# Another written order for a fused attention, gated bilinear and mixing kernel: exps, scores, adds, pieces and their banks

## The chip, the cores and the metric

The kernel runs on one core of a Trainium2 chip. The metric is the device time of one execution in microseconds. Three runs of the kernel before gave 643.65, 643.19 and 643.61 us, with a median of 643.61 us.

## The reference

The input x has 2,048 rows of 512. Attention with 32 heads of width 16 and a bilinear unit with 1,376 hidden columns work on the same x, and a gate per row mixes the two.

```python
def _A_ref(x, wqkv, wo):
    qkv = (x @ wqkv).reshape(B, S, 3, H, Dh).transpose(2, 0, 3, 1, 4)
    q, k, v = qkv[0], qkv[1], qkv[2]
    scores = jnp.einsum("bhqd,bhkd->bhqk", q, k) * (Dh ** -0.5)
    p = _softmax(scores, axis=-1)
    o = jnp.einsum("bhqk,bhkd->bhqd", p, v)
    return o.transpose(0, 2, 1, 3).reshape(B, S, D) @ wo

def _B_ref(x, w_gate, w_up, w_down):
    h = (x @ w_gate) * (x @ w_up)
    return h @ w_down

g = _sigmoid((x * gate_w).sum(-1, keepdims=True))
return g * _A_ref(...) + (1 - g) * _B_ref(...)
```

## The kernel before, in words

**Tiles and units.** Queries are handled in four chunks of 512 columns and heads in four groups of eight. A pass m (0 to 31) is one chunk, one group and every second head of the group, so four heads j. Keys come in 16 tiles kt of 128. A unit (m, kt, j) is one block of scores, 128 keys by 512 queries of one head; there are 2,048 of them. The scores of a unit are one matmul on a 32-row strip of TensorE, into a PSUM bank of its own (`do_row`, L786). An exp then turns the bank into a cell of the SBUF buffer `PT`, which has 58 cells of 512 columns (`do_exp`). ACT does 1,300 units with its exponential (L863). DVE does the other 748 as an integer addition whose result, read as a float of 16 bits, is a power of two with a straight line between the powers (L865). Two shifted copies of such a cell, which POOL makes with an integer addition (`do_add`, L883), are weighted into the value product, so that the error of the straight line averages out. An exp or an add can take two units in one instruction (three for ACT), if their banks are neighbours and their cells have one spacing; an add is a pair of instructions, one for each copy.

**Value products.** `do_pv` (L831) adds probabilities times values: four matmuls of 128 rows, one on each 32-column strip, for the four heads of the pass, into bank 7. There are 888 such rows with 3,544 matmuls: 2,048 with a plain cell and 1,496 with a shifted copy. The sums of the probabilities come out of the same products. Afterwards bank 7 is copied out (task `oc`), the sums are inverted and spread (tasks `dn`, `rc`, `rg`, `re`, `rb`) and multiplied in (task `mu`).

**Pieces.** Projections of x (names q, k, v, z), the bilinear unit (u, g) and the output (o) are works of several pieces each. A piece is four matmuls on the four column strips (`do_fill`, helper `mm_col`, L702). The work takes a bank with its first piece and gives it back when its result is copied out. A few pieces are instead cut in four row quarters and put among scores (L781).

**Order.** Nothing on the chip chooses the order. `SCHED` (L220 and following) is a packed text with one line for each operation. The loop behind L1115 unpacks it and gives each line to its function. The order of the lines is the order of each engine's instructions. Waits follow from the data: each operation carries what it depends on, and `_Plan.emit` writes the semaphores. `take_cell` (L848) makes an exp or an add wait for the last readers of a cell that it overwrites, and `bank_rel` makes a score or a first piece wait for the exp or copy that read its bank. The lines are:

- `R 0 m kt j bank`: scores of a unit (L786); `R 1 name piece quarter ...` is a quarter of a piece (L781).
- `F name piece [bank]`: a piece (L702).
- `V m a b c d`: a value product, with the key tile and the copy for each head (L831).
- `E engine m kt j cell ...`: an exp of one to three units (L863 for ACT, L865 for DVE).
- `A n ...`: an add of n units into 2n cells (L883).
- `T name engine`: a copy, a small operation or a DMA (`run_task`). `S` and `C` are three matmuls at the end.

At the end, after the last value product, DVE transposes bank 7 and inverts the sums (tasks `tx`, `tr`, `tg`, `ty`), TensorE spreads them with the selection matmuls `S` (L1143), DVE multiplies them in (tasks `tt`, L1098), and the last pieces of the four output works o30 to o33 (the sixteenth, with `Qr`) use the result.

Of the kernel before, what the change touches and what calls it, by code (L numbers as in the profile page):

```python
# [17 lines left out]
AX = mybir.AxisListType  # L18
# [186 lines left out]
def bass_gated_mix__mha_block__glu_gated_bilinear__prompt_kernel(  # L205
# [19 lines left out]
    "^*31uYUlTV??>?{*8y5}CDiW@`SjztkY=n{T(83SJ6%JF)?)qt=Oncy+TM@d3-#~!-Yf5I!WW>5iHHZdF#G}h>+^j7k3BSzuWkIXg3p4qNp%VdpTZ)p<VEMFL3|(j#TNXQk$i&|*u7$~"
    "adF_!z#lNDb0giizj+iOM**^Aou7i@w{@(6YilUJ9R<$&+BE6rdwQMC&KblF`oY!UU*lh|-WnY%NF*WZ#dHNV^%Q=;wfM?BV|w0o`+T?gUO(S#<a;@M0#$b|tULeM_t1X)e}DGAQ;h2R"
    "iF97j=7nF54HYjy^DdlPL46l%c&{73V{kA02B2s9ePcd#i<b_W@NX21n29?%==0%5_2i#{KicZ|R+uOq!ELxmT*&Zk=<JuUdVc$ENXHppujWDTN2}S|+umB$KrHxCThTbU@8#BdC_1b-"
    "OKc~FvwrE3Ss&ab`RR&Td1@hkU+z=)1ny&(JZhW#rit%=-&hSc6xhxy@PGTB*M)z4J_M^xrz4QrWAVb|Q&c-B3pB1Uf|2sm+q`1--I@bnW$rHtjF-If)?e`KsC)4CllL#hj=T4Q7Y*hw"
    "uh08<HtKbYJ@bh*>7NwSoU7EiYF(%+hP!&~LgOlrJ@wY0a1m>5-&OJXDM)Z~xPeU{R|o$(|0+^ruVden2(%K;M)3QyuDyY^U<^rh@2q8`3+pG?iof{r*g=9ozTbQTWh5AjACKNm(U{-t"
    "`kQ@Je=Wog7cvi_#rwuZFpL-HcK`CemI>ZbEZ_;#7f=TizTb@%KREvq=ywHti%8$C@%acb&3ZX~U+?QFz@OHGY4L2R?070YELj*Y)$Riu<T%5B?&$>)kiMk*B6-~UrGZKEet{pzy@U0S"  # L230
    "`AH5m>#y<ehz?%-egAg80%Ow1=#eeiEnoU0!Hn3Mn+jvlhQaItQM`BQ*n*T^5LWE6G0G<>$lqm)Uk?5qI;!JcDev4&nWvO?68pW2kEvueMHmUZSaAe@NoAdN{|)0K(qc^f`L3;c@ICil"
    "4aAt{%Q5Tz-P8(ppmc~FJHd(x;&j2IzpSms`~qz_Y7PpIe}t@#zX$&&*04msC8zII`n>=hGR*f6?{N?ax?_#h><-0A^Q)n<E{G@&rDL1hdl!eIg^3mRuDvI~xFGzlm&U#yeM@t3Zvp0f"
# [24 lines left out]
    "tfde&8Y6H){PmyQ?SFeeOZ6O<q&X}o#u)$xMriL}BhOvGjf6JTE3Y<cvYiR1m!2vQy;MT;E|B?o=-7C~-HA1@1X*S7o+09%H3%>KUP5OlwUaX)w5zF$Qfut-z3#)W`j%Tu6XsN(2f*gl"
# [215 lines left out]
T, KD, NCH, NB, FT = 16, 4, 4, 4, 11  # L473
# [816 lines left out]
```

## Time and profile before

| | |
|---|---|
| median of three runs | 643.61 us |
| span of the profiled execution | 641.4 us |
| PE busy | 634.8 us in 8,804 matmuls |
| ACT busy | 622.1 us in 837 instructions |
| DVE busy | 597.0 us in 927 instructions |
| POOL busy | 514.7 us in 1,185 instructions |
| granted TensorE clock | 1.000 |

The profiled execution's span runs from its first to its last instruction; its own device time is not listed apart from the three runs, which are 1.8 to 2.3 us longer than the span. PE is TensorE's matmuls and PEld its weight loads, which overlap the matmuls. A group's busy time leaves overlaps out, while its mean is that of single instructions, start to end. In the view of waits, an idle time names what ended it.

### The profile page before, as it was taken

The page shows a single profiled execution, that of the slowest core. Times are in us where ns is not written, and L with a number is a line of the kernel's source. Part 1 is how long each engine was busy: PE and PEld are TensorE (multiplying, and loading weights), DVE is VectorE, ACT ScalarE, POOL GpSimd, SP SyncE. Part 2 cuts the span into 40 slices and gives each one's busy share as a digit, 9 for nine tenths or more (in the row PEclk, how much of TensorE's full clock was granted, in tenths as well). Part 3 has the DMA queues.
Part 4 walks back from the last instruction along what each step waited for, and adds up shares of the span by engine and source line. Part 5 has one row for each costly group of instructions (what it writes and reads, how often), then busy time and mean ns, then how long its engine had stood idle before and what let it go on. Part 6 is the DMA issues. An engine that isn't in the chain of part 4 may idle for free.

```text
span 641.4 us, 21177 instructions
## 1 busy us (share of the span) xinstructions
PE 634.8 (99%) x8804; PEld 202.4 (32%) x8804; DVE 597.0 (93%) x927; ACT 622.1 (97%) x837; POOL 514.7 (80%) x1185
## 2 busy tenths in 40 slices
PE   8999999999999999999999999999999999999997
PEld 3333232223323322333232333323333223333233
DVE  6999999999999999999999799999998999999975
ACT  6999999999999999999999999999999999999994
POOL 2469899897978889797998789878688998888862
PEclk9999999999999999999999999999999999999999
DMA  8930211001010010101001010100101000000001
GB/s 154 287 100 3 68 15 31 17 6 30 12 28 4 20 43 3 37 10 34 4 11 38 10 43 12 30 9 5 33 4 44 19 23 16 4 26 3 28 20 37
DMA packets 30803, 21.17 MB, mean 33 GB/s; under 512 B 18632, under 2 KB 26540, under 8 KB 30704
## 3 DMA queue, kind: packets, MB, share of 16 engines
q1 hardware_dynamic: 29200, 18.75, 11.3%
q8 instruction: 69, 1.13, 0.7%
q10 hardware_dynamic: 1504, 1.05, 0.7%
q14 instruction: 30, 0.25, 0.1%
HBM read 11.64 MB, written 2.37 MB: 22 GB/s over the span
## 4 chain that ended last, share of the span: by engine, by line
PE 93%; DVE 4%; DMA 1%; ACT 1%; issue 0%; ACTq 0%; DVEq 0%
PE ps L831 35%; PE ps L786 29%; PE ps L702 28%; DVE PT L865 2%; DMA wa<-in_A_wqkv_dram 1%; ACT PT L863 1%; PE ps L781 1%; DVE wa L1027 0%; DVE usb L1019 0%; ACTq L559 0%; DVE QE L904 0%; DVE oc L904 0%; PE ps L1143 0%; DVE rec L1064 0%; DVE rec L1061 0%
## 5 line engine op out<-in xcount | busy, mean ns | idle before, releaser
L863 ACT ACTIVATE PT<-ps 128x1024 bf16<-128x1024 f32 (+2 forms) x823 | 615.3, 886 | 4.9 <-PE ps L786 2.6
L883 POOL INT64_ADD PT<-PT x1174 | 511.8, 457 | 113.7 <-DVE PT L865 73.2
L865 DVE TENSOR_SCALAR PT<-ps 128x512 int16<-128x512 f32 (+1 forms) x641 | 467.9, 773 | 26.7 <-PE ps L786 21.2
L831 PE MATMUL ps<-PT,V 128*32 128x512 bf16 (+1 forms) x2048 | 262.3, 384 | 0.0
L831 PE MATMUL ps<-PT,VS 128*32 128x512 f16 x1496 | 242.8, 384 | 0.0
L786 PE MATMUL ps<-QE,KK 32*128 32x512 bf16 x2048 | 237.4, 384 | 0.9 <-ACT PT L863 0.3
L786 PEld LDWEIGHTS ps<-QE,KK 32*128 32x128 bf16 x2048 | 64.8, 91 | 230.5 <-ACT PT L863 126.0
L831 PEld LDWEIGHTS ps<-PT,V 128*32 128x32 bf16 x2048 | 63.9, 95 | 62.6 <-issue 49.5
L831 PEld LDWEIGHTS ps<-PT,VS 128*32 128x32 bf16 x1496 | 59.2, 94 | 49.2 <-issue 32.1
L702 PE MATMUL ps<-xT,wg 128*32 128x512 bf16 x704 | 51.9, 382 | 0.1
L702 PE MATMUL ps<-xT,wu 128*32 128x512 bf16 x704 | 52.0, 382 | 0.0
L702 PE MATMUL ps<-wd,wa 128*32 128x512 bf16 x668 | 50.7, 382 | 0.0
L1027 DVE TENSOR_TENSOR wa<-ps,usb 128x512 bf16<-128x512 f32 x44 | 30.1, 685 | 1.3 <-PE ps L702 0.8
L1019 DVE TENSOR_TENSOR usb<-ps,omg 128x512 bf16<-128x512 f32 x44 | 30.1, 684 | 1.0 <-PE ps L702 0.7
L702 PEld LDWEIGHTS ps<-xT,wg 128*32 128x32 bf16 x704 | 15.5, 95 | 18.1 <-issue 6.3
L904 DVE COPY oc<-ps 128x512 f32<-128x512 f32 x31 | 21.1, 682 | 0.0
L702 PE MATMUL ps<-xT,wa 128*32 128x512 bf16 (+1 forms) x272 | 20.6, 379 | 0.5 <-DMA wa<-in_A_wqkv_dram 0.5
L702 PEld LDWEIGHTS ps<-wd,wa 128*32 128x32 bf16 x668 | 14.8, 95 | 19.1 <-issue 9.6
L702 PEld LDWEIGHTS ps<-xT,wu 128*32 128x32 bf16 x704 | 14.9, 95 | 17.9 <-issue 6.3
L702 PE MATMUL ps<-wo,OT 128*32 128x512 bf16 x240 | 19.9, 382 | 0.0
L702 PE MATMUL ps<-wa,xT 128*32 128x512 bf16 x256 | 18.1, 381 | 0.3 <-DMA wa<-in_A_wqkv_dram 0.3
L702 PE MATMUL ps<-xT,wq 128*32 128x512 bf16 x256 | 18.0, 388 | 0.0
(85 smaller groups left out, 148.2 us busy)
## 6 DMA issues: line engine op xcount, KB each, us to landing
rb<-rscr SPq DMA_DIRECT2D x16, 256.0 KB
QE<-Qr SPq DMA_DIRECT2D x120, 16.0 KB, 1.8
oc<-oc SPq DMA_DIRECT2D x60, 32.0 KB, 1.9
out_dram<-ost SPq DMA_DIRECT2D x12, 128.0 KB, 1.9
wu<-in_B_w_up_dram SPq DMA_DIRECT2D x1, 1376.0 KB, 7.2
wg<-in_B_w_gate_dram SPq DMA_DIRECT2D x1, 1376.0 KB, 11.8
wd<-in_B_w_down_dram SPq DMA_DIRECT2D x1, 1280.0 KB, 15.1
wa<-in_A_wqkv_dram ACTq DMA_DIRECT2D x1, 512.0 KB, 7.0
```

The source lines that it names most:

```text
L702: r = pe.matmul(ps[32 * i : 32 * i + 32, bank, 512 - x_.shape[1] : 512], w_, x_, start=s0, stop=s1, tile_position=(0, 32 * i), skip_group_ ...
L781: w.op = pe_op(lambda pe, lhs=lhs, rhs=rhs, r=r, q=q, bank=bank, s0=s0, s1=bool(last): pe.matmul(ps[:, bank, :], lhs[r, :], rhs[r, :], sta ...
L786: o = pe_op(lambda pe, b=b, kt=kt, j=j, p=p, bank=bank: pe.matmul(ps[:, bank, :], KK[32 * j : 32 * j + 32, b, kt * 128 : kt * 128 + 128], ...
L831: return pe.matmul(ps[32 * j : 32 * j + 32, OB, :], lhs, rhs, start=s0, stop=s1, tile_position=(0, 32 * j), skip_group_check=True)
L863: o = P.op("act", lambda a: a.activation(PT[:, cs, :], ps[:, bs, :], ACT.Exp, scale=math.log(2.0) / 1024.0), deps)
L865: o = P.op("dve", lambda v: v.tensor_scalar(PT[:, cs, :].bitcast(I16), ps[:, bs, :], BIAS16, 0.0, ALU.add, ALU.max), deps)
L883: return g.int64_add(PT[:, zl, :].bitcast(I64), PT[:, src, :].bitcast(I64), PH[r] * 0x0001000100010001)
L904: return lambda v: v.tensor_copy(dst, src) if scale is None else v.tensor_scalar(dst, src, scale, None, ALU.mult)
L1019: return fill_op(key, "dve", lambda v: v.tensor_tensor(usb[:, i % 2, :], ps[:, bank, :], omg[:, cf, :], ALU.mult), d)
L1027: return fill_op(key, "dve", lambda v: v.tensor_tensor(hT[:, f, :], ps[:, bank, :], usb[:, i % 2, :], ALU.mult), d)
```

## The change

Only the text in `SCHED` is new; no function is touched. As a diff it is 256 packed lines taken out and 242 put in, of which nothing can be read. Unpacked, the orders have 6,374 and 6,259 lines. The operations of each kind:

| | before | after |
|---|---|---|
| exps on ACT of one, two, three units | 363, 443, 17 | 468, 392, 16 |
| exps on DVE of one, two units | 534, 107 | 508, 120 |
| units on ACT, on DVE | 1300, 748 | 1300, 748 |
| adds of one, two units (two instructions each) | 426, 161 | 122, 313 |
| scores | 2048 | 2048 |
| value products, their matmuls | 888, 3544 | 888, 3544 |
| pieces whole, quarters | 780, 52 | 781, 48 |
| tasks | 552 | 552 |

733 of DVE's 748 units are the same, the pieces keep their order within some 15 places, and scores stand some 20 places from where they stood among the scores. Nearly every value product joins other key tiles. Each exp and each add has new cells: in the order before, a cell is used again long after its last reader, in the new one often right behind it.

The packed lines look like this in the diff:

```diff
 SCHED = (
...
-    "{rFo_z~}4V{{hrjDW?"
...
 )
```

Unpacked, the first lines that differ:

```diff
-E act 0 0 2 0 0 0 0 1
+E act 0 0 2 0 0 0 0 57
...
-E act 0 0 1 2 0 0 3 3
+E act 0 0 1 55 0 0 3 56
...
-E act 0 2 1 13 1 0 0 14
-E dve 0 1 2 15
-F k01 1 6
+E dve 0 1 2 3
+E act 0 3 3 6
```

Adds in pass 7, before and after:

```
A 1 7 4 1 33 17
A 1 7 1 2 1 4
```

```
A 2 7 1 3 7 7 0 27 56 42 48
```

The end, from the last value product to the last sixteenth piece, before (two lines that the steps of the end speak of are the `S` lines and `F o31 15`):

```
V 31 43 39 45 22
T tx dve
F o33 0
T oc31 act
T tr dve
T tg dve
T ty0 dve
T dn31 sp
T ty1 dve
F o32 14
...
S 0 4
S 1 3
T tt0 dve
T tt1 dve
F o33 3
F o33 10
F o30 15
F o31 15
F o32 15
F o33 7
F o33 6
F o33 15
F o33 5
```

and after:

```
V 31 38 45 45 -
T tx dve
F o33 5
T ce4 dve
T tr dve
T tg dve
T oc31 act
T ty0 dve
F o33 10
...
S 0 4
T dn31 sp
T ty1 dve
S 1 3
T tt0 dve
F o31 15
T tt1 dve
F o30 15
F o33 6
F o32 15
...
F o33 15
F o33 13
```

More of the change, by code (lines that the diff above doesn't have):

```diff
@@ L225 @@
[L225 to L232, printed above, removed]
@@ L469 @@
[L469 to L470 removed]
+    "c-n0JTdplRjxC7(S1V=*jzgp*dwlxGJq<`4tpAFLja@(@)5|?8&IO|NwTxqs9JaII8$QjJnMo8ykrc(p|NQ(p#>YO#|M5TLYVz0lJHCJa{ki|x_tpRP8K2F+<P+oX{6GHJ=g0Ra|L5l)|NF;t{qN89"
+    "|M~a-hkyTD{Qcj)TX_ES?;i5nKC7;ucJg|D_l0(%ng8GOe}0@V@AJF&|NXo=aAEl2-7|{+ZQmUjE`~H>pS`o2<LT%7{f5v2C;!G5MnUV}cN2~A$G_YB{*K@5Rb5O%`h2o6Dtqu)qy5Ig_XxAU2j~Y1"
+    "3n;#7h%prB6n$Uh7|@nwI|@eNC1FoY8z8K{A53RU>_6V#?8ou*OzVHyZzE^*`%k#~{v$yBe(m{g;KK0Jn0|WNyFhpd==bV!fB$Qc8Z|LE0dIVkH2D4ARpXnl8Sokvo*e*Z29X-E_*@PCI)7)NJU-#X"
@@ new lines @@
+    "8~!VZ=BFpo2`MHZ$n?7xVq-mj1m#-)ZQ#f8)3^_+Ib{eFlbLhuNj%>;5TZPucMAruWwQez4?HXS?ry%nzn{)`;5m`BW0|3Mv~=O6i66($2=uJ)Zs+HY=C`btGdj%~u}@C-uJvpm&`5UsfZv0DzTbhM"
+    "BT$}iJp;BT_@{{jZ%zF08<#o%{=x#lLjc^-c>>bQ`7Dga{C?x*yS+2kWp?_E;T90aLwxbp#19ytf5?2!7-f#@8=7Y}{%h4@d0sU^|My+bT|>5Ftoe7V`8_`KqZs*y`IOeaKLj<N#YVor_RlTr;sDD7"
+    "D9+zmKtDaNha>*i*~|WUB^x}xTeI(0bCwU8{T0h0LG?oJ@e9$}v+lpKb$#qb75?yw9Ni(biKgvYS3m#%f90~eK%W=p;vx&ZWah7@*_v&yH3RX2>+6&2|Ni(hW8eRO+Ph;u8k+AREMZFDsCV|Trp&oN"
+    "6d0d7ekPDv%;4^o3(5KbeZQ9L15)DDqN~0!A%JLLSq*StffyKV;uS3nz5gEZB`|;gVev!f@8oZBK$F!REqdYD>#aK_RlL3w&~IWrsvR&98;KKBN%}N0PyTuG7wc?>NX&seJ<nA%*0gs8@9(J_xyp=#"
@@ new lines @@
+    "FL0gg(pvD^74-f6|4ZSwXVo-_-(x-qk_kZbp<w)Z@;5lZ&H0bTG=)Ns_f(Hh3rnwQUmuEA^MGDvGDK)ElKDCL-r%qE7bN~YvN;|ypQCUvdy>64W!#u>!cb+lEY|Nf3h)`Em(T8B=q)6s(Bt#=H~j_P"
+    "o3T8veJ`JH2DC~?aLmT{y;D#?;(cTH8|w2JMLzNrpWhhymK@(RG}z3;ho`-iBnNALy8Z6(`OkUxu>5bfOoiZk_Wb!*>u>9H?a~UK1*H01$pf3I#2G1J6<hr;^X3W$IwE}0*a8gSK+Wgh=4-8oD9)qH"
+    "T`=z5>sA!2S$r>^s4R-nZ13Sbya32uf%g;W@jJdGx?+O9r_DfS>%*<U189%3*ZCq^mQrzmI14@#{U;gGQax{hg~<2*P4)?E&BoK&4k}rE81oJW^9}YxLgOKm7)kJ_?|**w^bVa-<#-QDV^zO)4I>p{"
+    "+adg9nR-fQTZId1S(f_M(?1A%DW%Q_xy@nhSz5{RTD=d{2{GEI7x;Kj^LV)HGcl`}(sMmtBIpP~mJNq`_UEH0hm!OsRp&pcN<Y8Gu|S@EUp%|EFHY+D2uqtfg%$*LLwwd4RQJN|!Vc0D(Ls=<W!jrI"
@@ new lines @@
+    "0)KdR%Z@TyGi5>#?E>-N%;I_$+BZ>sv61Ur+JDao6kmU+{+mLVDu$Mu7XwEV9?|M%z;l#_eM3dVvlaaHTS(Xty_c<R=ab3b(KI|$0(~=D54bHkW-Qz5kxl>W^N(+=eSi30|2JE3B?5n_iY>1EHWtM9"
+    "(C31Pjuz}`;dd^a;E80&#uXZC?VACQ;NN!*_G#8Fk>Itj+Om`$w%1c+qLzi!kZ-IvT`RZC|88%hMbn<``sNr$V4=1-fh2I(?@4_m&h;#bU;`&-dxA8+iD2!AKo%I@_f60NbiV4<p1I%v{OX>bF?f-;"
+    ">8`DpsD<7zi=LlF{e^k_?*4luYsCy=0~=572c!qBlTW6O&LCa?`1>!|31L|Kokr*t_$;)~26A&j)^KJsUV!?LgXlfRy>%#bU);TaZyDlxhE8u+txj)^vS`A{c5>>1{CMrS{_*dYj4S>;`xSG{bn4L$"
+    "t;>GNDEb4*w=7G?Mk@EgVzaS9YK!KlHg9Pw3W#@%F-Y(Zj{dZ3;496nW?}uTy@`Qb*}(Ns<apzGhQ5Wj&Uo#3+Wmfa0c$ZcN?eIr=Z-hWcES>nGhl@D5#gY7K=F{5e?k{~X4AQ~c&<#)_6y;8>K*>s"
@@ new lines @@
+    "op)*KRv~6>EjiSobAQs&tA#NOR2~prUuY{ToWVZ1Q5R6XEBDKf;#D!$vg{hZjAbu5vI)W25bTe?$jlf}#fH*d>uL`PFtenx(4Bmi^=@Y>D#0TwW5UDlevw-n+qdq@vH+g)mx+`x0Zd&Kc&;nOx(yS$"
+    "@Ma7eHj@=#$=R+{ZL=<;XP6t(;{|O>JL9DcdQ-vbFt%inyWE;~B%bWiPURq&rlSCzrt>#5G-l^&Dom%V`A$<B6l~PieRexbhFo%R=VANJLpo!0Zm}z*$GDrsM8coxkg{o5GYt~otS_C|and;KS@sr3"
+    "bipNbr>KFJx<FFRF8`mou{;u55^x5tb0MFit#pEJ+mfg~ggR1Q(Wy4&&Zf0(o<c#c&MK@It4mTB=*&3IO~$d(4F<r6XjYUB=Ip+;7IC8DN>JzB(yPeu_-GpK>^;4lwb-9!6~NzRf^wyVG9>mj^kHXq"
+    "u-*$f*Ej+@IkYIW5Os1Ou3ql(=)CFo$Y4CaI`X1Et^qRdOEW`z*&gDoz4-59sQizgCTTyd3VsIzxmmhAE=OL}UzBCf&nzm&;rtT0alAr!ce-|iwcH&NPoyQrU}f4aMtB04W}Pz&frTZs%7)tUk<=^)"
@@ L471 @@
+    "W$ni6nm_w;C%Z2f6~B0UV~FwXKRfy2M%dr1_jo<;ew?@W;~xr2<@o"
 )
```

457 lines of the change are left out of this document (216 added, 241 removed).

## The prediction

> **What bounds the kernel now.** I read the page's first part and the chain that ended last, then the groups by shape, then PE's timeline.
>
> ```profile
> span 641.4 us, 21177 instructions
> PE 634.8 (99%) x8804; PEld 202.4 (32%) x8804; DVE 597.0 (93%) x927; ACT 622.1 (97%) x837; POOL 514.7 (80%) x1185
> PE 93%; DVE 4%; DMA 1%; ACT 1%; issue 0%; ACTq 0%; DVEq 0%
> PE ps L831 35%; PE ps L786 29%; PE ps L702 28%; DVE PT L865 2%; DMA wa<-in_A_wqkv_dram 1%; ACT PT L863 1%; PE ps L781 1%; DVE wa L1027 0%; DVE usb L1019 0%; ACTq L559 0%; DVE QE L904 0%; DVE oc L904 0%; PE ps L1143 0%; DVE rec L1064 0%; DVE rec L1061 0%
> ```
>
> 93% of the chain is PE: the value products (L831), the scores (L786) and the pieces of the projections (L702). ACT is busy nearly as long, so it is a second bound close behind. Busy shares do not tell which of them gives way, because matmuls overlap; the distances between PE's starts do.
>
> ```profile
> 300.16 0.38 PE L831 MATMUL ps<-PT,V 128*32 128x512 bf16 x1
> 300.48 0.39 PE L786 MATMUL ps<-QE,KK 32*128 32x512 bf16 x3
> 300.80 0.39 PE L831 MATMUL ps<-PT,V 128*32 128x512 bf16 x2
> 301.02 0.39 PE L831 MATMUL ps<-PT,VS 128*32 128x512 f16 x4
> 301.36 0.40 PE L786 MATMUL ps<-QE,KK 32*128 32x512 bf16 x4
> 301.69 0.40 PE L831 MATMUL ps<-PT,V 128*32 128x512 bf16 x4
> 301.93 1.05 PE L702 MATMUL ps<-xT,wu 128*32 128x512 bf16 x16
> ```
>
> Two kinds of work alternate. A column step is four matmuls on four column strips (a row V, or a piece F). A score stretch is a run of rows R on different row strips. From column step to column step it takes 0.22 us (300.80 to 301.02; the four steps at 301.93 last 1.05, less one matmul of 0.39 gives 0.22 for each of three). Into a stretch it takes 0.32 (300.16 to 300.48), out of it 0.32 (300.48 to 300.80), and a stretch of three scores costs what one of four does (301.36 to 301.69 is 0.33). So PE's time is a count of steps and of stretches, not of matmuls; I use 0.216 and, for a stretch with both its edges, 0.642.
>
> The written order before has 1,094 steps from column to column, 572 stretches, and 31 second rounds inside longer stretches, where a row strip comes again (one more step each). That is 1,094 x 0.216 + 572 x 0.642 + 31 x 0.21 = 236.3 + 367.2 + 6.5 = 610.0 us.
>
> ```profile
> 6.13 1.40 PE L702 MATMUL ps<-xT,wq 128*32 128x512 bf16 x16
> 632.07 0.38 PE L831 MATMUL ps<-PT,VS 128*32 128x512 f16 x1
> 633.79 0.60 PE L702 MATMUL ps<-wo,OT 128*32 128x512 bf16 x8
> 634.33 1.13 PE L1143 MATMUL ps<-usb,sel 128*128 128x256 f32 x4
> 635.39 0.61 PE L702 MATMUL ps<-wd,wa 128*32 128x512 bf16 x8
> 635.83 0.82 PE L702 MATMUL ps<-wo,Qr 128*32 128x512 bf16 x12
> 637.12 0.39 PE L702 MATMUL ps<-wd,wa 128*32 128x512 bf16 x4
> ```
>
> From the first piece at 6.13 to the last at 637.12 are 631.0 us; less 610.0, and less 1.4 for the selection matmuls (634.01, which is 633.79 and a step, to 635.39), some 19.6 us are left. This leftover, 3% of the span, is all the waiting that PE does, and all that any reordering without fewer stretches can win.
>
> **The change, part by part.** The count of units, of value products and of tasks stays. What moves are the counts below, read from the two written orders.
>
> PE. Steps go from 1,094 to 1,097, stretches from 572 to 570, second rounds from 31 to 30: +3 x 0.216 - 2 x 0.642 - 0.21 = -0.85 us. At the end, after the last value product, 17 pieces follow in place of 18 and the selection comes after eleven of them in place of nine, so that its DVE result is needed directly: the sixteenth piece of o31 stands right behind the second selection matmul. Before, two plain pieces at 635.39 stood between.
>
> ```profile
> 635.06 0.86 DVE L1098 TENSOR_TENSOR Qr<-ps,oc 128x256 bf16<-128x256 f32 x2 [0.52 <-PE ps L1143]
> ```
>
> The first of these two products starts 0.73 after the selection's first matmul (634.33) and lasts 0.43 (half of 0.86): 1.16 plus a handover of some 0.05 as an estimate from the gaps above, against 1.06 (634.33 to 635.39) after which PE is free. So PE waits 0.15 there, and the PE part is -0.85 + 0.15 = -0.7 us.
>
> Exps. ACT's singles go from 363 to 468, doubles from 443 to 392, triples from 17 to 16; DVE's singles from 534 to 508, doubles from 107 to 120. Units per engine stay at 1,300 and 748.
>
> ```profile
> L863 ACT ACTIVATE PT<-ps 128x1024 bf16<-128x1024 f32 x443 | 428.1, 1064 | 3.2 <-PE ps L786 2.0
> L863 ACT ACTIVATE PT<-ps 128x512 bf16<-128x512 f32 x363 | 201.5, 638 | 1.7 <-PE ps L786 0.6
> L863 ACT ACTIVATE PT<-ps 128x1536 bf16<-128x1536 f32 x17 | 25.6, 1506 | 0.1
> L865 DVE TENSOR_SCALAR PT<-ps 128x1024 int16<-128x1024 f32 x107 | 130.2, 1219 | 3.8 <-PE ps L786 3.2
> L863 ACT ACTIVATE PT<-ps 128x512 bf16<-128x512 f32 x10 | 5.0, 641 | 0.0
> L863 ACT ACTIVATE PT<-ps 128x1024 bf16<-128x1024 f32 x17 | 15.8, 1061 | 0.0
> 130.25 3.07 DVE L865 TENSOR_SCALAR PT<-ps 128x512 int16<-128x512 f32 x5
> ```
>
> The means overstate it, for instructions overlap their successors. In two stretches of like exps back to back (fifth and sixth row), ten singles take 5.0, so (5.0 - 0.64) / 9 = 0.48 each, and seventeen doubles 15.8, so (15.8 - 1.06) / 16 = 0.92 each. ACT's own load becomes 105 x 0.48 - 51 x 0.92 - 1 x 1.38 (a double and half of one) = +2.1 us. By the groups' busy time (201.5 / 363 = 0.555, 428.1 / 443 = 0.966, 1.506) it would be +7.5, but that counts waiting starts as work; I take 2.1, since ACT does run back to back (it idles 5.0 us before all 823). DVE: singles are (3.07 - 0.68) / 4 = 0.60 apart, so -26 x 0.60 + 13 x 1.217 = +0.2: nothing. The Trainium skill, "Perfetto Trace Analysis", section "Optimizing Scalar/DVE Operations", gives a fixed cost per instruction on PSUM data of about 51 ns for Scalar and 125 ns for DVE. By it ACT would gain 53 x 0.051 = 2.7 us of load and DVE lose 1.6. The trace agrees for ACT (2 x 0.48 - 0.92 = 0.04) and not for DVE (2 x 0.60 - 1.217 is below zero).
>
> On the path, ACT's 2.1 us is costed at nothing, because ACT's own sum lies below PE's: 363 x 0.48 + 443 x 0.92 + 17 x 1.38 = 605 us before, 607 after, inside the 621 between first and last exp (below). If that cover is gone, it costs 2.1.
>
> ```profile
> L863 ACT ACTIVATE PT<-ps x823: 592/1020/1612, 9.5 to 630.9; 128x1024 bf16<-128x1024 f32 x90, 128x512 bf16<-128x512 f32 x71, 128x1536 bf16<-128x1536 f32 x4
> ```
>
> Banks and the leftover. PE waits where a bank's exp ends late.
>
> ```profile
> PEld ps L786 <- ACT PT L863: 126.0, 310, 0.8
> PEld ps L786 <- DVE PT L865: 61.5, 151, 0.6
> PEld ps L786 <- issue: 26.2, 67, 0.4
> PEld ps L831 <- POOL PT L883: 8.4, 36, 0.5
> ```
>
> Most of these idle times are the plain edge of a stretch: 0.391 us where nothing held it (26.2 / 67), against 0.407 with an exp named (187.5 / 461). The excess is 461 x 0.016 = 7 us, the part of the leftover that exps cause at a stretch's first score; the rest sits inside stretches, at the start and in tenths of steps. Which sign does the new order give it? I counted, in both orders, how many of the some 2,045 bank returns leave under 0.05 us beyond the shortest chain (score 0.38, exp, two handovers): 309 before, 329 after. Doubles on DVE are the cause: 185 of theirs were that tight, 208 are. If the whole leftover went with tight returns, that is 20 / 309 x 19.6 = +1.3 us. If it went with returns of one engine and margin at the trace's rate for them, the split ones, which come back sooner, offset the doubles: -0.2 to +0.4. I take +0.1, since the excess named above is only a third of the leftover.
>
> Adds. POOL's instructions fall from 1,174 to 870: 122 single and 313 double pairs in place of 426 and 161.
>
> ```profile
> L883 POOL INT64_ADD PT<-PT x1174 | 511.8, 457 | 113.7 <-DVE PT L865 73.2 <-DVE OT L1078 21.1 <-PE ps L831 7.0
> ```
>
> POOL idles 113.7 us before its adds, so at most 304 x 0.457 = 139 us less work there is worth nothing. A merged pair delivers its first copy later, by up to one add's 0.457; the cover is the distance in PE's order from the scores to the product that reads a copy, whose shortest twentieth rises from 2.9 to 3.1 us. Without that cover the price is the 36 waits above, 8.4 us with their edges, doubled at worst.
>
> Cells. 181 exps now write a cell of PT whose last reading value product stands behind their own scores; before it was 2. They wait one edge (0.32) longer than for the scores, if the engine is idle then. ACT idles 5.0 us over 823 exps, so it is at the previous exp still; zero is taken, and 181 x 0.32 = 58 us of delayed starts is what is uncovered if the engines were waiting.
>
> Sum: -0.7 + 0.1 = -0.6 us on a span of 641.4. The three runs had a median of 643.61 us; the 2.2 between lies around the recorded instructions and is untouched by the order. So 643.61 - 0.6 = 643.0.
>
> **The rivals.** *ACT becomes the bound (slower).* Its place is every stretch in which ACT's load exceeds PE's steps, its price 2.1 us, and it decides if ACT's 14 us beyond its sum (621 - 607) cannot be spent because each gap is shorter than an exp. For it: ACT idles 5.0 us in all. Against it: PE holds 93% of the chain, ACT 1%. PE's saving then counts for nothing: 643.61 + 2.1 = 645.7. The same section of the Trainium skill advises grouping operations when the engine is saturated, and "TensorEngine Tiling (Array Packing)", section "PSUM Bottleneck", says that PSUM copies may become the limit once tiling has sped up TensorE; splitting goes against both, and the trace bears them out as far as ACT's 97%.
>
> *Sooner returns shrink the waiting (faster).* 51 more doubles are split, and a split exp gives its first bank back 0.43 us (1.064 - 0.638) sooner. If a third of the 7 us goes, the time is 643.61 - 0.7 - 2.3 = 640.6. For it: 461 stretches stood behind an exp. Against it: the count of tight returns does not fall.
>
> *The reordering touches nothing* (643.6): margins are equal and waits are jitter of exps. It falls into the forecast's own range.
>
> **How the numbers follow.** What runs of this kernel can tell from no change is about 0.2%, 1.3 us: 642.3 to 644.9. The forecast with its bounds, -0.7 - 0.2 to -0.7 + 1.3, is 642.7 to 644.2 and lies inside; chance 0.44. Sooner returns 0.33, ACT as the bound 0.23. The range reaches from 640.4 (640.6 and the 0.2 that the returns may give) to 646.1 (645.7 and the 0.4 that they may cost); what is left out is a halving of the waits, and ACT at its busy-time price of 7.5.
>
> **What would show it.** In the profile after, ACT's singles keep 0.48 and doubles 0.92; the excess of stretches behind an exp stays at 7 us, give or take 2; PE keeps over 90% of the chain; POOL's idle time grows past 113.7 without PE waiting for it more. Wrong would be: ACT taking several per cent of the chain, stretches waiting longer than 0.407 behind ACT, or exps waiting for L831, which this trace does not show.

## The result and the profile after

The kernel after takes 647.25 us (median of four runs, 646.33 to 648.37) against 643.61 us before. The ratio is 1.0058 with a 95% interval of 1.0044 to 1.0072, so it is slower by 3.6 us, or 0.6%. The forecast of 643.0 us had the sign wrong, and the range (640.4 to 646.1) misses the median by 1.15 us. The profiled execution took 647.01 us. The lines of the code stand 14 earlier than before (L863 is now L849, L865 L851, L883 L869, L831 L817, L786 L772, L702 L688, the product `mu` L1064, and the DMAs on SP: `od` L1041, `re` L1055, `rb` L1060, `dq` L961).

The first part of the page after, and its chain that ended last:

```profile
span 644.3 us, 21223 instructions
PE 634.8 (99%) x8804; PEld 198.0 (31%) x8804; DVE 597.0 (93%) x914; ACT 624.2 (97%) x890; POOL 466.2 (72%) x881
PE 76%; ACT 13%; SPq 3%; DMA 3%; DVE 3%; issue 1%; ACTq 0%; POOL 0%; DVEq 0%
PE ps L817 27%; PE ps L688 25%; PE ps L772 24%; ACT PT L849 13%; SPq L961 2%; DVE PT L851 1%; DMA oc<-oc 1%; DMA wa<-in_A_wqkv_dram 1%; DMA rscr<-rec 1%; SPq L1041 1%; PE ps L767 1%; SPq L1060 0%; SPq L1055 0%; DVE OT L1064 0%; ACTq L545 0%
```

PE is as busy as before, to the tenth, in a span 2.9 us longer. But it holds 76% of the chain where it held 93%. ACT's exps went from 1% to 13%, and new names are SP's queue and the DMAs behind it: `oc<-oc` (task `od`) and `rscr<-rec` (task `re`), with the issues of `dq`, `od`, `rb` and `re`. The view of groups by shape shows ACT's load:

```profile
L849 ACT ACTIVATE PT<-ps 128x1024 bf16<-128x1024 f32 x392 | 384.5, 1095 | 2.2 <-PE ps L772 1.7
L849 ACT ACTIVATE PT<-ps 128x512 bf16<-128x512 f32 x468 | 257.5, 663 | 3.9 <-PE ps L772 3.1 <-POOL PT L869 0.2
L849 ACT ACTIVATE PT<-ps 128x1536 bf16<-128x1536 f32 x16 | 24.3, 1518 | 0.1
```

The mean of a single rose from 638 to 663 ns, of a double from 1064 to 1095. The view of one line's instructions gives the first and the last start of all exps on ACT:

```profile
L849 ACT ACTIVATE PT<-ps x876: 592/768/1699, 9.2 to 633.8; 128x512 bf16<-128x512 f32 x87, 128x1024 bf16<-128x1024 f32 x84, 128x1536 bf16<-128x1536 f32 x5
```

From 9.2 to 633.8 are 624.6 us. The prediction's pitches make ACT's own sum 607 us, so 17.6 us are left; before, 621.4 less 605 left 16.4. ACT has 2 us more to do, and the time that it leaves unused did not get smaller. The waits (us in total, times, longest):

```profile
PEld ps L772 <- ACT PT L849: 136.6, 327, 0.5
PEld ps L772 <- DVE PT L851: 60.4, 144, 0.9
PEld ps L772 <- issue: 20.9, 53, 0.4
PEld ps L688 <- ACT PT L849: 13.4, 50, 0.4
PEld ps L817 <- POOL PT L869: 9.1, 39, 0.3
DVE OT L1064 <- DMA oc<-oc: 2.9, 3, 1.3
```

A stretch whose bank an exp had held now waits (136.6 + 60.4) / (327 + 144) = 0.418 us, where it was 0.407, and 0.394 (20.9 / 53) where nothing held it. By the prediction's reckoning the excess is 471 x 0.024 = 11 us in place of 7. Pieces behind ACT (L688) wait 50 times and 13.4 us, before 31 and 7.4. And DVE stands at `mu` for `od`'s copies, which it did nowhere before.

The same can be counted from PE alone. I took every column step's and every stretch's start distance in both traces and subtracted what it takes when nothing is waited for (0.216 for a step, 0.32 into and 0.321 out of a stretch; these smallest distances are the same in both traces). What remains is PE's waiting: 22.0 us before, 25.7 after, which is +3.7. The written order has 0.85 us less of steps. +3.7 - 0.85 is the 2.9 us by which the span grew; as waiting is what remains, this sum closes by construction. What it shows is the split: the steps came down as counted, and the waits rose by more.

One of the new waits from end to end. SP's issues, then DVE, then PE, around the product `mu` of block 4 in the timeline after (start, duration; in brackets the idle time before it and what ended it):

```profile
227.40 0.66 SPq L1060 DMA_DIRECT2D rb<-rscr  x1
228.10 0.55 SPq L961 DMA_DIRECT2D QE<-Qr  x1
228.69 1.22 SPq L1041 DMA_DIRECT2D oc<-oc  x2
...
231.82 0.69 DVE L1064 TENSOR_TENSOR OT<-oc,rb 128x512 bf16<-128x512 f32 x1 [1.17 <-DMA oc<-oc]
232.43 1.28 DVE L851 TENSOR_SCALAR PT<-ps 128x512 int16<-128x512 f32 x2
...
232.16 0.39 PE L772 MATMUL ps<-QE,KK 32*128 32x512 bf16 x2
233.17 0.38 PE L772 MATMUL ps<-QE,KK 32*128 32x512 bf16 x1 [0.62 <-DVE PT L851]
```

The last two `od` copies of the block are issued from 228.69 on; an `od` takes 2.0 us from issue to landing (median of the page). `mu` stands next on DVE and waits 1.17 us for them. The exp at 232.43 stands behind it in DVE's order and starts only then, and PE's score at 233.17 waits for that exp's bank. Before, the last of these DMAs was issued well ahead:

```profile
225.22 0.66 SPq L1074 DMA_DIRECT2D rb<-rscr  x1
...
230.16 0.68 DVE L1078 TENSOR_TENSOR OT<-oc,rb 128x512 bf16<-128x512 f32 x1
```

Here are 4.9 us between the last issue and `mu`; after, 2.5 (231.82 less some 229.3). It happens in blocks 2, 4, 6 and 11: DVE stands 0.37, 1.17, 0.43 and 1.28 us (for the 0.37 the trace names no releaser, for the others `od`), and PE's distances are 0.36, 1.00, 0.33 and 0.90 us too long there, 2.6 us together.

### The profile page after: what moved, and what is told of

Its sections match the earlier page's. It is cut to its first block, busy times and chain, and to the rows that moved or that the text cites. A ratio compares the mean times of both kernels' runs of the same rounds, so it can differ in the third digit from the quotient of the medians.

```text
span 644.3 us, 21223 instructions
## 1 busy us (share of the span) xinstructions
PE 634.8 (99%) x8804; PEld 198.0 (31%) x8804; DVE 597.0 (93%) x914; ACT 624.2 (97%) x890; POOL 466.2 (72%) x881
## 3 DMA queue, kind: packets, MB, share of 16 engines
q1 hardware_dynamic: 29200, 18.75, 11.3%
## 4 chain that ended last, share of the span: by engine, by line
PE 76%; ACT 13%; SPq 3%; DMA 3%; DVE 3%; issue 1%; ACTq 0%; POOL 0%; DVEq 0%
PE ps L817 27%; PE ps L688 25%; PE ps L772 24%; ACT PT L849 13%; SPq L961 2%; DVE PT L851 1%; DMA oc<-oc 1%; DMA wa<-in_A_wqkv_dram 1%; DMA rscr<-rec 1%; SPq L1041 1%; PE ps L767 1%; SPq L1060 0%; SPq L1055 0%; DVE OT L1064 0%; ACTq L545 0%
## 5 line engine op out<-in xcount | busy, mean ns | idle before, releaser
L849 ACT ACTIVATE PT<-ps 128x512 bf16<-128x512 f32 (+2 forms) x876 | 617.5, 872 | 6.1 <-PE ps L772 4.8
L869 POOL INT64_ADD PT<-PT x870 | 463.3, 552 | 165.6 <-DVE PT L851 88.4
L851 DVE TENSOR_SCALAR PT<-ps 128x512 int16<-128x512 f32 (+1 forms) x628 | 467.9, 786 | 25.9 <-PE ps L772 19.7
L817 PE MATMUL ps<-PT,V 128*32 128x512 bf16 (+1 forms) x2048 | 259.0, 384 | 0.0
L772 PE MATMUL ps<-QE,KK 32*128 32x512 bf16 x2048 | 237.7, 384 | 1.8 <-DVE PT L851 1.4
L817 PE MATMUL ps<-PT,VS 128*32 128x512 f16 x1496 | 207.2, 384 | 0.0
L772 PEld LDWEIGHTS ps<-QE,KK 32*128 32x128 bf16 x2048 | 63.9, 91 | 237.0 <-ACT PT L849 136.6
L817 PEld LDWEIGHTS ps<-PT,V 128*32 128x32 bf16 x2048 | 61.3, 95 | 63.5 <-issue 49.6
L817 PEld LDWEIGHTS ps<-PT,VS 128*32 128x32 bf16 x1496 | 49.7, 95 | 45.7 <-issue 28.2
L688 PE MATMUL ps<-wd,wa 128*32 128x512 bf16 x672 | 54.5, 382 | 0.1
L688 PE MATMUL ps<-xT,wu 128*32 128x512 bf16 x704 | 52.7, 382 | 0.3
L688 PE MATMUL ps<-xT,wg 128*32 128x512 bf16 x704 | 52.5, 382 | 0.1
L688 PE MATMUL ps<-wo,OT 128*32 128x512 bf16 x240 | 22.5, 381 | 0.7 <-DVE OT L1064 0.7
L688 PEld LDWEIGHTS ps<-wd,wa 128*32 128x32 bf16 x672 | 15.3, 95 | 19.3 <-issue 10.1
L688 PEld LDWEIGHTS ps<-xT,wu 128*32 128x32 bf16 x704 | 15.0, 95 | 19.4 <-issue 5.9
L688 PEld LDWEIGHTS ps<-xT,wg 128*32 128x32 bf16 x704 | 15.2, 95 | 18.7 <-issue 6.1
L688 PE MATMUL ps<-xT,wa 128*32 128x512 bf16 (+1 forms) x272 | 20.2, 378 | 0.6 <-DMA wa<-in_A_wqkv_dram 0.6
L688 PE MATMUL ps<-xT,wq 128*32 128x512 bf16 x256 | 18.3, 381 | 0.4 <-ACT xT L637 0.3
L688 PE MATMUL ps<-wa,xT 128*32 128x512 bf16 x256 | 17.4, 381 | 0.3 <-DMA wa<-in_A_wqkv_dram 0.3
```

The lines of the kernel that those rows point to most:

```text
L688: r = pe.matmul(ps[32 * i : 32 * i + 32, bank, 512 - x_.shape[1] : 512], w_, x_, start=s0, stop=s1, tile_position=(0, 32 * i), skip_group_ ...
L772: o = pe_op(lambda pe, b=b, kt=kt, j=j, p=p, bank=bank: pe.matmul(ps[:, bank, :], KK[32 * j : 32 * j + 32, b, kt * 128 : kt * 128 + 128], ...
L817: return pe.matmul(ps[32 * j : 32 * j + 32, OB, :], lhs, rhs, start=s0, stop=s1, tile_position=(0, 32 * j), skip_group_check=True)
L849: o = P.op("act", lambda a: a.activation(PT[:, cs, :], ps[:, bs, :], ACT.Exp, scale=math.log(2.0) / 1024.0), deps)
L851: o = P.op("dve", lambda v: v.tensor_scalar(PT[:, cs, :].bitcast(I16), ps[:, bs, :], BIAS16, 0.0, ALU.add, ALU.max), deps)
L869: return g.int64_add(PT[:, zl, :].bitcast(I64), PT[:, src, :].bitcast(I64), PH[r] * 0x0001000100010001)
```

## The experiments

Two theories came out of this. **L**: ACT's load is paid at nearly its full price, because its gaps are waits for scores and cannot be spent. **T**: the tasks' DMAs were moved on SP, and DVE stands at `mu`. The rival of both is that the time lies in cells, adds or in the order as such. All kernels but the three named `short` compute everything. The last column has the time of the kernel before, measured beside each.

| kernel | edit | us (lowest to highest) | ratio to before, 95% | before beside it |
|---|---|---|---|---|
| od_early | after, `od` earlier on SP | 648.0 (647.01 to 650.33) | 1.0057 to 1.0086 | 643.71 |
| od_before_rb | after, seven `od` into SP's wait | 645.79 (645.0 to 646.52) | 1.0025 to 1.0052 | 643.4 |
| mu_early_before | before, `mu` earlier | 656.36 (654.96 to 657.49) | 1.0184 to 1.021 | 643.71 |
| mu_late | after, `mu` later | 648.03 (647.56 to 648.41) | 1.0056 to 1.0084 | 643.67 |
| mu_late2 | after, two `mu` later, no add crossed | 647.93 (646.42 to 648.91) | 1.0053 to 1.0079 | 643.65 |
| before_unchained | before, `mu` free of POOL | 643.9 (643.17 to 644.96) | 0.9999 to 1.0017 | 643.37 |
| after_unchained | after, `mu` free of POOL | 648.11 (646.95 to 648.47) | 1.0058 to 1.0085 | 643.37 |
| split_before | before, 53 ACT doubles split | 645.36 (644.84 to 645.95) | 1.0015 to 1.0036 | 643.71 |
| split_before_3x | before, 159 split | 650.46 (650.29 to 650.57) | 1.0093 to 1.0124 | 643.4 |
| merge_before | before, 28 pairs of singles merged | 649.75 (649.67 to 649.94) | 1.0081 to 1.0111 | 643.67 |
| merge_before_far | before, 47 merged, new cells | 655.4 (654.89 to 655.5) | 1.0166 to 1.0194 | 643.67 |
| od_merge | od_before_rb, 29 merged | 651.61 (650.05 to 652.5) | 1.0101 to 1.0132 | 643.67 |
| before_short | before, ACT 8 columns less | 642.47 (642.11 to 642.72) | 0.9973 to 0.999 | 643.65 |
| after_short | after, ACT 8 columns less | 643.44 (642.26 to 645.02) | 0.999 to 1.0007 | 643.65 |
| od_short | od_before_rb, ACT 8 columns less | 642.69 (640.12 to 644.02) | 0.9975 to 0.9993 | 643.65 |
| cells_far | after, cells given out anew | 647.15 (645.88 to 647.51) | 1.0043 to 1.0071 | 643.4 |
| adds_single | after, double adds split | 698.08 (697.5 to 699.7) | 1.0834 to 1.0862 | 643.71 |
| adds_single_far | cells_far, double adds split | 693.69 (692.75 to 694.86) | 1.0768 to 1.0798 | 643.4 |

**The load of ACT: splits.** In the order before, every eighth and then about every third double on ACT becomes two singles in the same place:

```diff
-E act 0 6 3 43 0 5 1 44
+E act 0 6 3 43
+E act 0 5 1 44
```

> The order before, with 53 of ACT's 443 double exps, evenly spread, written as two singles each; cells, banks and all else as before. Theory L: ACT gets 53 x 0.04 to 0.05 = 2.1 to 2.7 us more load and has no slack, so 645.7 to 646.3 us. Theory T: ACT's gaps take it up, 643.6 us within 0.6. Rival of sooner returns: below 643 us.

> The order before with 159 doubles of ACT written as two singles, three times as many as in split_before. If ACT is the bound throughout, each split costs its 0.04 to 0.05 us, so +6.4 to 8 us, 650.1 to 651.7 us. If the 1.65 us of split_before scales, +5.0, 648.7 us. If ACT's gaps take up the splits, under 646 us.

53 splits cost 645.36 - 643.71 = 1.65 us, 159 cost 650.46 - 643.4 = 7.06: 0.031 and 0.044 us each. Two singles less a double is 0.477 x 2 - 0.904 = 0.050 us of ACT's time, by the smallest regular start distances in both traces. So a split costs six tenths of what it adds to ACT at the first dose and nine tenths at the second. The first time lies a little under the 645.7 to 646.3 us of theory L, the second inside its 650.1 to 651.7. Nothing else was moved in the order, though a split also gives its first bank back sooner and its second one 0.05 us later. The change has 53 more instructions on ACT. The page of the run with 159:

```profile
PE 640.7 (99%) x8804; PEld 204.5 (32%) x8804; DVE 599.5 (93%) x927; ACT 630.2 (97%) x996; POOL 514.9 (80%) x1185
PE 72%; ACT 24%; DVE 1%; DMA 1%; issue 0%; ACTq 0%
```

ACT's share of the chain went from 1% to 24% by splits alone, while its busy share stayed at 97%.

**The load of ACT: merges.** If each additional exp costs 0.03 to 0.04 us, each one less should give it back, and a merged order before might beat both kernels. Neighbouring singles on ACT became one double, at the place of the second:

```diff
-E act 0 3 1 18
...
-E act 1 2 2 28
+E act 0 3 1 18 1 2 2 28
```

> Before, with 28 pairs of neighbouring single exps of ScalarE written as one double, nothing else. Theory L: 28 by 0.031 to 0.044 us less, 642.3 to 642.7 beside 643.5, faster than both kernels. Rival S (a merged exp waits for the later bank, before's split is the better one): 643.4 to 644.5.

> Before, with 47 pairs of neighbouring single exps of ScalarE written as one double, and the PT cells given out again so that the cell that was free longest comes first (a double needs its two cells in rising order). Theory L: 47 by 0.031 to 0.044 us less, 641.4 to 642.1 beside 643.5. Rival S: 643.4 to 645. If new cells cost something of themselves, which a run on after did not show (647.15 against 647.25), it lies above merge_before by that.

> After, with the od copies moved as in the run od_before_rb (645.79 us there), and 29 pairs of neighbouring single exps of ScalarE written as one double. Theory L (each exp more on ScalarE costs 0.031 to 0.044 us, so each less gives that back): 29 of them are 0.9 to 1.3 us, the time comes to 644.5 to 644.9. Rival S (the price holds only upwards: fewer exps give nothing back, since a merged exp waits for the later of its two banks): 645.5 to 646.2.

All three missed, and not only L's figure: the time rose by 6.1, 11.7 and 5.8 us, some 0.2 us for each merge, beyond what the rival allowed. Two lines of the waits of merge_before, with L846 and L769 for the exps and the scores:

```profile
PEld ps L685 <- ACT PT L846: 10.4, 32, 0.7
ACT PT L846 <- PE ps L769: 8.1, 25, 0.5
```

ACT now waits 25 times and 8.1 us for scores (10 times and 2.6 us before), for a double cannot start until its later bank is filled; then it gives both banks back at its end, and pieces behind ACT wait up to 0.7 us (before 0.4). So the number of exps cannot be lowered without touching when banks return, and a merge is no test of load. The load had to be varied in another way.

**The load of ACT with the order kept.** ACT's exps take 504 of the 512 columns of each unit, once a cell has been written; units, banks and order are the same, and each operation waits for the same others:

```diff
-                o = P.op("act", lambda a: a.activation(PT[:, cs, :], ps[:, bs, :], ACT.Exp, scale=math.log(2.0) / 1024.0), deps)
+                w = 504 if filled.issuperset(cells) else 512
+                o = P.op("act", lambda a: a.activation(PT[:, cs, :w], ps[:, bs, :w], ACT.Exp, scale=math.log(2.0) / 1024.0), deps)
```

> Before, with ScalarE's exps over 504 of the 512 columns of each unit once the cell has been written (the last 8 columns keep what stood there, which is left out of the computation); order, units and banks unchanged. 1300 units by 8 columns by 0.834 ns (a double's pitch less a single's, 0.904 - 0.477 us, over 512) are 8.7 us less on ScalarE. Theory L (ScalarE's load is a bound beside TensorE, what it does not do comes back until the waits behind it are gone; before has some 3.9 us of them): 639.5 to 642 beside 643.6. Rival S (TensorE alone sets the time and the waits are those of order): 643.0 to 643.8.

> The same 8 columns left out of ScalarE's exps in after (8.7 us less on ScalarE). Theory L: after has some 9.2 us of waits behind ScalarE's banks, so it gains more than before does: 641 to 644, and the distance to before_short shrinks from 3.6 us to the 1.4 to 2.6 us of VectorE standing at mu. Rival S (the distance is the order itself): 646.5 to 647.5, or a fall like that of before, with 3 to 4 us of distance left.

> After, with the od copies moved as in od_before_rb (645.79 us) and the 8 columns left out of ScalarE's exps. If VectorE's standing at mu and ScalarE's load are all of the 3.6 us, it lies within 1 us of before_short. If a third part is in it (other waits of the new order), it stays more than 1 us above.

The same 8.7 us less on ACT give 1.2 us in before and 3.8 us in after. The 3.6 us between the two kernels shrink to 643.44 - 642.47 = 1.0 us, and with the `od` copies moved as well (od_short) to 0.2 us. So about 2.6 us of the difference are waits that a relieved ACT takes away; L's figures for after were met, before gained less than L gave it, and the distance left was smaller than the 1.4 to 2.6 us expected. The relief of 8.7 us is more than three times what the change adds to ACT, so it shows that the 2.6 us go by way of ACT, and not that the 53 instructions alone make them. The chains, first of before_short, then of after_short, then of od_short:

```profile
PE 94%; DVE 3%; DMA 1%; POOL 1%; issue 0%; ACTq 0%; DVEq 0%
```

```profile
PE 85%; DVE 4%; DMA 4%; SPq 3%; ACT 2%; issue 1%; ACTq 0%; DVEq 0%
```

```profile
PE 93%; DVE 2%; DMA 2%; ACT 1%; SPq 1%; issue 0%; ACTq 0%; DVEq 0%
```

With ACT relieved, ACT is gone from after's chain (13% to 2%) while SP's queue, the DMAs and DVE keep their 10%. With the copies moved too the chain is nearly that of before; but the profiled execution of od_short, with 640.12 us, is the fastest of its eleven runs, so its chain may show the copies at their best. These are two causes side by side, and each shrinks with its own edit. The runs of after_short and od_short spread over 2.8 and 3.9 us, so the 0.2 is not known better than to some 0.8 us.

**DVE at `mu`: the copies.** The first attempt put all `od` of blocks 2, 4, 6 and 11 right behind `dn` on SP, ahead of `re` and `rb`:

```diff
 T dn5 sp
+T od2.0 sp
+T od2.3 sp
+T od2.2 sp
+T od2.1 sp
```

> The order after, with the four row copies (tasks od) of the blocks 2, 4, 6 and 11 moved forward on SP's queue to stand right behind the DMA of the same block's sums; nothing else moves. Theory T (DVE stands at the products mu, which wait for copies issued late on SP; PE loses the stalls that follow): the four waits of 0.4 to 1.3 us before mu go, and with them the PE stalls of 0.36, 1.00, 0.33 and 0.90 us that the trace after has there, so about 647.2 - 2.6 = 644.6 us. Rival L (ACT is the bound, and the 53 more exps are what costs): no change, 647.2 us, the waits before mu go all the same.

The time did not fall: 648.0 us, which these runs cannot tell from after's 647.25. The waits tell why:

```profile
DVE OT L1064 <- DMA rb<-rscr: 3.4, 4, 1.4
PE ps L772 <- DMA QE<-Qr: 1.2, 1, 1.2
```

`mu` needs `rb` as well. With `od` ahead of it on the queue `rb` came later, and the wait changed its name without going. In block 4 the `od` also stood ahead of `dq` copies that the next scores need, and PE waited 1.2 us for one, which it did nowhere in after. So seven of the `od` were moved only into the place where SP waits ahead of `rb` or stands just before it:

```diff
 T re4.0 sp
+T od4.3 sp
+T od4.2 sp
```

> The order after, with the late row copies (od) of the blocks 2, 4, 6 and 11 moved only into the time in which SP waits for the landing of re ahead of rb, so that neither rb nor a copy is later than before; od_early had moved the wait from od to rb. Theory T (DVE stands at mu for a DMA): no wait of mu for a DMA is left in the trace and the PE stalls at 152, 232, 305 and 494 us go, 647.3 - 2.6 = 644.7 us. Theory L (53 more exps on ACT are all of it): 647 us. Both together (split_before gave 1.65 of the 3.6 us): 644.5 to 645.5 us.

645.79 us, 1.5 us less than after (the ratios to before are 1.0038 and 1.0058, and their intervals just overlap). Cells_far, the order of after with other cells, was timed beside it and took 647.15 us, 1.4 us more. The time lies between T's 644.7 and L's 647, a little above the 644.5 to 645.5 for both together. Its waits at `mu`, and its chain:

```profile
DVE OT L1064 <- DMA rb<-rscr: 1.0, 3, 0.6
```

```profile
PE 76%; ACT 19%; DVE 1%; issue 1%; DMA 1%; ACTq 0%; POOL 0%
```

The waits for `oc<-oc` are gone, 1.0 us for `rb` is left, and the chain keeps only ACT beside PE. T is worth about 1.4 us here, known to some 0.5 us.

**DVE at `mu`: moving the product.** If `mu` stands too early for its copies, it can be moved later; and in before, moved earlier, it should make the same wait.

> The order before, with the products mu of the blocks 2, 4, 6 and 11 moved forward on DVE's queue, to where their last copy has not landed yet (by some 0.4, 1.2, 0.4 and 1.3 us as an estimate from the issue times). Theory T: DVE stands there for about 3 us in all and PE loses 2 to 3 us, so about 646 us. Theory L: no change, 643.6 us.

> After, with only the four products mu of blocks 2, 4, 6 and 11 moved later on VectorE: two instructions later in 2, 4 and 6, one in 11; every DMA stays where it is. Theory T (part of the 3.6 us is VectorE standing at mu for copies that SP issued late): the 0.37, 1.17 and 0.43 us of standing go and about half of the 1.28 us of block 11, of TensorE's 2.6 us of stalls at these places some 1.4 to 2.1 us go, the time comes to 645.2 to 645.9 and no wait for oc over 0.8 us is left. Rival A (the whole 3.6 us is ScalarE's 53 additional instructions): no change, 646.9 to 647.6.

Both missed. mu_early_before cost 12.7 us, not 2 to 3; mu_late came out 0.8 us above after instead of 1.4 to 2 below it, though these runs cannot tell 0.8 from nothing. The waits of mu_late:

```profile
DVE OT L1064 <- POOL PT L869: 1.5, 2, 0.8
```

No wait for a copy is left, but two for POOL. The code has a chain that I had passed over: `mu` waits for the last add written ahead of it, and the next add waits for `mu` (the list `alone` in `do_add` and in the task). In blocks 2 and 6 the move took `mu` past adds. PE's stalls there grew from 0.36 and 0.33 to 1.27 us each, the one of block 4 (1.00) went, and the one of block 11 fell from 0.90 to 0.82, because a piece stood right behind that needs `mu` itself. That is +0.91 + 0.94 - 1.00 - 0.08 = +0.8 us at these places; the whole span of the profiled execution is 0.4 us longer than after's, so that the 0.8 of the medians agrees is in part luck. The same chain is part of mu_early_before, where `mu` waited 3.4 us for adds besides 3.4 us for DMAs (1.8 for `rb`, 1.6 for an `od`). Behind its four products PE's distances are 2.8, 2.2, 1.9 and 1.7 us too long, 8.6 of the 11.3 us by which its span grew; the rest is not accounted for. So `mu` was moved again, in blocks 4 and 6 only and past no add:

> After, with the products mu of blocks 4 and 6 alone moved later on VectorE (behind two exps and behind one), with no add of GpSimd crossed, to which mu is chained in both directions. Theory T: TensorE's stalls of 1.00 us at 232 and 0.33 us at 305 go, 645.9 to 646.4 beside after's 647.25. Rival A (VectorE standing at mu costs nothing by itself): 646.9 to 647.6.

Missed again: 647.93 us. The stall of block 4 is gone. In block 6 the timeline shows POOL:

```profile
305.40 6.01 POOL L869 INT64_ADD PT<-PT  x10 [4.25 <-DVE OT L1064]
```

`mu` ran later, so POOL's next ten adds stood 4.25 us for it. A value product at 307.37 came 0.35 us late behind one of them, an exp of ACT at 309.16 stood 0.54 us for another, and the stretch of five scores at 309.92 took 1.38 us up to the next product, where the same one takes 0.78 in after. In block 2, which was not touched, `mu` waited 1.0 us in this execution and PE 0.95 (0.36 in after's). The moment at which copies land differs between executions, and the kernel feels it where `mu` stands close behind them. Last, the chain itself was taken away in both kernels:

```diff
-                o = P.op("pool", fn, [cell_op[u + (0,)] for u in us] + [d for q in z for d in take_cell(q)] + [c["add0"]] + [d for d in alone if d.eng == "dve"])
+                o = P.op("pool", fn, [cell_op[u + (0,)] for u in us] + [d for q in z for d in take_cell(q)] + [c["add0"]])
...
-                                 [done[f"rb{cb}"]] + [done[f"od{cb}.{j}"] for j in range(4)] + ot_out(cq, b) + alone)]
+                                 [done[f"rb{cb}"]] + [done[f"od{cb}.{j}"] for j in range(4)] + ot_out(cq, b))]
...
```

> Before, with the products mu (and the last one, te) no longer ordered against GpSimd's adds: GpSimd's next add does not wait for mu, mu does not wait for the add ahead of it. mu's operands and result share no memory with the adds. GpSimd stood 21.1 us behind mu here and mu itself waited for nothing, so theory G (the chain costs TensorE time through late adds): 642.5 to 643.4 beside 643.6, after's the larger fall. Rival V (GpSimd has the time, only VectorE's standing counts; or adds beside mu are slower and give it back): 643.4 to 644.2.

> After with the same chain taken away. mu still waits for its copies (3.25 us in all in the profiled run), GpSimd's 17.7 us of waits behind mu go. Theory G: the part of mu's cost that goes by late adds returns, 645.5 to 646.8 beside 647.25. Rival V: the stalls behind VectorE stay as they are, 646.9 to 647.6.

643.9 and 648.11 us: nothing came back, as rival V had it (after_unchained even lies above its 646.9 to 647.6). POOL's 21.1 and 17.7 us of standing behind `mu` cost nothing that these runs can tell, in the orders as they are. After_unchained also shows T's price at one place more plainly, since `mu` of block 4 waited longer there:

```profile
231.83 0.69 DVE L1064 TENSOR_TENSOR OT<-oc,rb 128x512 bf16<-128x512 f32 x1 [1.71 <-DMA oc<-oc]
```

DVE stood 1.71 us and PE's distance was 1.54 too long; in after it was 1.17 and 1.00. At this place PE loses nearly what DVE does.

**Cells and adds.** The cells of after were given out anew, the one that has been free longest first; then every double add was split into two singles, in after and in that kernel:

```diff
-A 2 0 7 3 0 1 1 3 33 17 30
+A 1 0 7 3 3 17
+A 1 0 1 1 33 30
```

> The order after, line for line, but with cells given anew: each exp and add takes the cells that have been free longest (a median of 53 lines between the last reader and the new exp). Theory T and L: exps and value products did not wait for cells, so 647.2 us within 0.7. Rival C (cells used again at once hold ACT, DVE or POOL): 644 us or less, and POOL's 32 us of waits for value products fall below 10.

> The order after, with all 313 double adds written as single ones in place, so 1,174 instructions on POOL as in the order before. Theories T and L: no change, 647.2 us within 0.6, and POOL's idle time falls. Rival (the merged pairs deliver their copies late and hold value products): some tenths to 2 us faster.

> The kernel of cells_far with the 313 double adds written as single ones. adds_single took 698 us. If that was POOL's own load (626 more instructions than double ones would be, 748 x 2 x 0.373 = 558 us, in bursts), it stays above 680 us. If it was the wait for cells used again at once, which holds the adds behind it, it falls to 650 us or less.

New cells changed nothing (647.15 us), so the 181 exps that write a cell close behind its reader are harmless. The adds missed what was expected: +51 us. From adds_single, POOL's group and the wait behind it:

```profile
L869 POOL INT64_ADD PT<-PT x1496 | 562.1, 398 | 118.8 <-DVE PT L851 60.2 <-PE ps L817 35.7 <-DVE OT L1064 13.9
...
PEld ps L817 <- POOL PT L869: 56.1, 126, 1.4
```

1,496 single adds are 562 us of POOL against 463 in after and 512 in before, and value products wait 56.1 us for them (9.1 in after). Some 4 of the 51 us go with other cells (693.69). That says where POOL's edge lies, and that the new order leans on its merged adds; it does not say that merging them brought anything over before, whose waits behind POOL were 8.4 us.

## Why the prediction was wrong, step by step

**The steps of PE: right, but for 0.2 us.** The steps are the -0.85 us that were counted. The pause of 0.15 at the end came too: from the second selection matmul to o31's sixteenth piece PE lost 0.46 us, where it lost 0.31 before the next plain piece in before. What the sum left out is that the selection itself comes later: its first matmul starts 0.51 us after the piece ahead of it, in before 0.32.

**The step that failed: "On the path, ACT's 2.1 us is costed at nothing, because ACT's own sum lies below PE's".** A sum inside a window is cover only if the engine can work in the gaps. ACT's gaps are mostly waits for scores: of 23.1 us above the smallest start distances in before, 19.8 stood before an exp whose scores had just come; in after it is 20.7 of 23.8. More load shifts ACT later and takes its banks along, and the gaps come again behind the next scores. The runs put 1.65 to 2.6 us in place of nothing: 53 splits alone, in the places of before, cost 1.65 us, and 2.6 is the 3.6 us of distance less the 1.0 us left with ACT relieved. Whether the microsecond between them is the place of the singles or the different meeting of ACT and PE stays open. The term was also a little small: by the smallest start distances (0.477, 0.904 and 1.331 us for a single, double and triple) 105 singles more, 51 doubles and a triple less are +2.65 us, where the prediction had 2.1, since its two stretches were not quite back to back.

**The rival "ACT becomes the bound" was the right mechanism.** Its price of 2.1 us lies inside the 1.65 to 2.6 us that was found, but its 645.7 us is still 1.6 us short, for it knew nothing of the tasks. Its sentence "each gap is shorter than an exp" named the condition. The evidence against it, that PE holds 93% of the chain and ACT 1%, was misread: the chain names who was last in that execution, not how close the next one is. split_before shows it, where the splits cost 1.65 us and ACT's share only goes from 1% to 2%, and split_before_3x, where ACT has 24%. The row that spoke for it, ACT idle 5.0 us in all, was on the page; by start distances ACT left 23 us unused. What it had not foreseen is that PE's saving still counts, since ACT bounds in some stretches only.

**The term that was missing: the tasks.** The sum has no row for SP's DMAs and none for `mu`. The prediction said that the count of tasks stays, and left their places out. Four of the 15 products had lost the lead of their copies; that is 1.4 us by od_before_rb, up to 2.6 by PE's stalls in the trace. 2.6 + 1.4 - 0.85 + 0.15 and the 0.2 at the selection are 3.5 of the 3.6 us. With the 0.75 us that moving the copies brings between after_short and od_short in place of 1.4 it is 2.85, so the sum is good to under a microsecond and no better.

**Banks: the count was right and the waits were not.** +0.1 us for tight returns stood for returns that leave no margin. The excess of stretches behind an exp rose from 7 to 11 us all the same, because returns that had margin lost it when ACT ran later. Where PE's start distances are over 30 ns too long, and the last thing to end before was an exp or copy on ACT, they add up to about 4 us in before and about 9 in after; behind DVE it is about 5 in both. The same sum behind ACT is about 6 us in split_before, 13 in split_before_3x, 11 in merge_before, and 2.4 and 2.9 in before_short and after_short: it rises and falls with the times of these kernels.

**Sooner returns: fell as a cause of gain.** A split does give its first bank back sooner, but before's splits cost time at both doses.

**Adds and cells: right at zero**, POOL's idle time grew from 113.7 to 165.6 us, and the value products' waits behind it stayed at 9.1 us in 39, where they were 8.4 in 36. The bound of the cells, 58 us, was not needed.

Of what would show it wrong, two came: ACT with several per cent of the chain, and stretches behind an exp at 0.418 (behind ACT alone 136.6 / 327, the same). Exps waiting for L817 did not.

No kernel that computes everything beat the one before.

## What to carry to other kernels

When a second engine is busy for 97% of the span and its gaps are waits for the first, cost what it gets more to do at most of its full price (six to nine tenths here), and look at who waits for it rather than at its share of the chain. When an order is rewritten, list for each task the issue of its DMA, the instruction that needs it and the lead between them, and what stands behind that instruction on its engine. To test a load, change the size of the instructions and keep their order: splitting, merging and moving them change when buffers come back, and moving an instruction crosses dependencies that its operands do not show.

## What the runs showed of the hardware that was not expected

The price of load is not even: 8.7 us less on ACT gave 1.2 us in before (0.14 us per us), while the splits cost 0.031 / 0.050 = 0.6 and 0.044 / 0.050 = 0.9 us per us. By these two kinds of edit the kernel before stands near a knee between PE and ACT. The Trainium skill, "Perfetto Trace Analysis", section "Optimizing Scalar/DVE Operations", gives 51 ns for each Scalar instruction on PSUM data, and the 0.050 us agree with it. What the section says of a saturated engine, that grouping operations can improve throughput, did not come true in this order, where 28 merges cost 6 us; the merges also moved exps and the return of banks.

A product on DVE with two operands in SBUF can take longer beside POOL's adds. The view of the line of `mu`, first in after, then in after_unchained (shortest, median, longest ns):

```profile
L1064 DVE TENSOR_TENSOR OT<-oc,rb x15: 681/682/694, 82.1 to 613.7; 128x512 bf16<-128x512 f32 x15
```

```profile
L1064 DVE TENSOR_TENSOR OT<-oc,rb x15: 679/683/1099, 81.6 to 613.5; 128x512 bf16<-128x512 f32 x15
```

Free of the chain two of the 15 last 1.08 and 1.10 us. Both lie wholly beside adds of POOL; three others that do so took 0.68 to 0.70. The same section of the Trainium skill says that GpSimd and DVE share an SBUF read port; the two longer products agree with that. It cost no time that these runs can tell from the kernels with the chain.
